# Attention, gated mix and feed-forward on one core: loads and dummy products ahead of the small vectors, a planner whose engines are free before their results, and later due times for gates and keys

## The chip, the cores and the metric

One Trainium2 chip, one core. Time is device microseconds (us) of one launch, the median of several runs; lower is better.

## The reference, cut to what matters

```python
# q, k, v: batch 2, 8 heads, 768 positions, head size 64; n_global 8, n_local 96
rel = pos[:, None] - pos[None, :]
keep = (pos[None, :] < n_global) | ((rel >= 0) & (rel < n_local))
scores = q @ k.T / 8 - slope_h * where(is_global & ~is_local, n_local, abs(rel))
a = softmax(where(keep, scores, -1e9)); x = a @ v          # 1536 tokens x 512
xk, xr = mu * x + (1 - mu) * x_prev                        # one mu for keys, one for gates
x = sigmoid(xr @ w_r) * (relu(xk @ w_k) ** 2 @ w_v)        # 512 -> 1024 -> 512
out = x + relu(layernorm(x) * g_ln @ w_ch1) @ w_ch2        # 512 -> 2048 -> 512
```

Weights are 64-bit floats. Each 128 x 512 piece is loaded as pairs of 32-bit words, turned into a 32-bit float and split into a high and a low part; the large products add high x high, high x low and low x high.

## The kernel before, in words

Tokens stand in 12 blocks of 128 (two batches of six). A block's attention is done in two halves of four heads, 24 half-blocks in all. In a block's first position the band of keys is 128 wide, elsewhere 232 (global 8, local 96, own 128). The steps of a half-block: transposition of q and k (`plan_turn`, L438; the copies out of PSUM are L445 on DVE, which multiplies by a scale tile `qs`, and L337 on ACT); scores (`plan_scores`, L484); adding the bias and taking the least (L495, DVE; it reads the bias tiles `nb0` or `nb`); exponent and sum (L501, ACT); transposition of the weights (`plan_weighted`, L519); one copy of them out of PSUM (L337 on ACT, tile `yy`); products with the values (L534). `plan_out` scales and transposes (L569). Then come, for six groups of 256 tokens, the gates' products (`plan_r`, L720, two halves of six per 128 tokens), the keys' products (`plan_k`, L756, eight of twelve), the values' products (`plan_v`, L793 to L795), and last the feed-forward half (L1047, L1141 to L1157).

Most work is recorded as operations with their engine, an estimated duration, what they read and write, the buffers they need and a due time. `Plan.play` then sets the order: it keeps a time for each engine (`CLOCK` holds the first ones), and always takes the operation that can start soonest by its estimates, the one with the earlier due time where several can. What it takes is issued at once, so it fixes every engine's instruction order, and the order of the loads on SP's queue. Its times steer nothing on the chip, where an engine goes on as soon as its semaphores let it.

The start is written by hand: eight memsets of `qs` and one of a 128 x 512 tile on POOL, ten dummy products on that tile (`warm_up`, L246), index tables on POOL (L265), the bias for the first block (`nb0`, L254 to L285, DVE, which needs the two counts that `words` loads), three loads of small vectors on SP's queue (L307). The bias for the other blocks (`nb`, L288 to L294) is one planned operation. `outside_band` (L67 to L87, twelve small DVE instructions) checks the counts; it is planned with a very late due time, and goes where DVE is free by the plan.

Of the kernel before, what the change touches and what calls it, by code (L numbers as in the profile page):

```python
# [8 lines left out]
F32 = mybir.dt.float32  # L9
F32R = mybir.dt.float32r  # L10
I32 = mybir.dt.int32
AF = mybir.ActivationFunctionType
ALU = mybir.AluOpType
# [3 lines left out]
P = 128  # L17
# [15 lines left out]

CLOCK = {"PE": 8.0, "ACT": 8.0, "DVE": 9.5, "POOL": 8.0, "SP": 2.5}
T0, STEP = 10.0, 5.0
CONV0, CONV1 = 20.0, 7.0
CONV2, CONV3 = 105.0, 5.0
K0 = 85.0  # L40
LOW, LATE_LOW = {"POOL": 1440}, {"DVE": 715}
TS = S // 2
PAIRS = 8
UP, LEAD = 15.6, 10.0
WARM = 10
SCALE = 0.125
BIG = 2.0**38
SM_EPS = 1e-9
# [7 lines left out]
def words(nc, a, tile_):  # L56

    w = tile_([P, 2, 2], "words", I32)
    for i, n in enumerate(("n_global", "n_local")):
        (nc.scalar, nc.gpsimd)[i].dma_start(w[:, i, :], a[n].bitcast(I32).rearrange("(o n) -> o n", o=1).to_broadcast([P, 2]))  # L60
    return w


# [46 lines left out]
class Plan:  # L110
# [4 lines left out]
    LAG = 70.0  # L115

    SWITCH = 95.0

    def __init__(self, clock):
        self.clock = {e: 1000.0 * t for e, t in clock.items()}  # L120
# [21 lines left out]
    def play(self):  # L142
# [13 lines left out]
        while open_:  # L156
            best = None
            for i in open_:
                engines, _, _, rooms, due, _, _ = self.ops[i]
                at = ready[i]  # L160
                ok = True
                for x in rooms:
                    if x.tile is None:
                        if live.get(x.tag, 0) < x.bufs:
                            f = free.setdefault(x.tag, [0.0] * x.bufs)
                            at = max(at, f[0])
                        else:
# [12 lines left out]
            t, _, i, e = best  # L180
            engines, fn, _, rooms, _, size, way = self.ops[i]
            for x in rooms:
                if x.tile is None:
                    live[x.tag] = live.get(x.tag, 0) + 1
                    free[x.tag].pop(0)
                    x.tile = x.make()
            self.now = t
            fn(e)
            end = t + engines[e]
            if e == "PE" and way != mode:  # L190
                end += self.SWITCH
                mode = way
            self.clock[e] = end
            if size:
                dma = max(dma, end) + size / 190.0
                end = dma + 1900.0
            trace.append((t, end, e, i))
            for x in rooms:
                x.left -= 1
                x.end = max(x.end, end)  # L200
                if not x.left and not x.hold:
                    live[x.tag] -= 1
                    free[x.tag].append(x.end + self.LAG)
# [11 lines left out]
class Fast:  # L215
# [23 lines left out]
    def warm_up(self):  # L239
# [1 line left out]

        ps = self.bank(7)
        y = self.t([P, 512], "cv", F32R, bufs=2)
        self.nc.gpsimd.memset(y.bitcast(F32), 1.0)
        for _ in range(WARM):
            self.nc.tensor.matmul(ps, y[:, 0:P], y, start=True, stop=True)  # L246

    def constants(self):
# [2 lines left out]

        nc = self.nc
        f = self.t([P, 2], "low")
        nc.vector.tensor_copy(f, self.words[:, :, 0])  # L254
        ng, nl = f[:, 0:1], f[:, 1:2]


# [18 lines left out]
        self.nb, self.nb0 = z[:, 0:C], z[:, C : C + P]  # L276
        o = slice(0, P)
        nc.vector.tensor_scalar(M[:, o], R[:, o], 0.0, None, ALU.is_ge)
        nc.vector.tensor_scalar(G0, J, ng, None, ALU.is_lt)
        nc.vector.scalar_tensor_tensor(L[:, o], R[:, o], nl, M[:, o], ALU.is_lt, ALU.mult)  # L280
        nc.vector.tensor_tensor(M0, G0, L[:, o], ALU.max)
# [4 lines left out]
        yield  # L286
        o = slice(P, C)
        nc.vector.tensor_scalar(M[:, o], R[:, o], 0.0, None, ALU.is_ge)  # L288
        nc.vector.scalar_tensor_tensor(L[:, o], R[:, o], nl, M[:, o], ALU.is_lt, ALU.mult)
        for x in firsts:  # L290
            nc.vector.tensor_scalar(L[:, x], R[:, x], ng, None, ALU.is_lt)
            nc.vector.tensor_scalar(R[:, x], R[:, x], 0.0, nl, ALU.mult, ALU.add)
        nc.vector.tensor_scalar(M, L, -BIG, BIG, ALU.mult, ALU.add)
        nc.vector.tensor_tensor(self.nb, R, M, ALU.add)  # L294

# [3 lines left out]
            self.nc.gpsimd.memset(self.qs[(h % 2) * D : (h % 2 + 1) * D, h // 2, :], -SCALE / slope(h))  # L299

    def small_params(self):
        nc, a = self.nc, self.a
        self.mhalf = self.t([P, 1], "mhalf")
        nc.vector.memset(self.mhalf, -0.5)
        self.vec = self.t([P, 5, 4], "vec")
        for i, n in enumerate(("moe_mu_k", "moe_mu_r", "moe2_g_ln")):
            nc.sync.dma_start(self.vec[:, i, :], a[n].rearrange("(c p) -> p c", p=P))  # L307
        nc.vector.tensor_scalar(self.vec[:, 3:5, :], self.vec[:, 0:2, :], -1.0, 1.0, ALU.mult, ALU.add)

    def part(self, tags):  # L310

# [151 lines left out]
    def plan_scores(self, i):  # L463
# [26 lines left out]
        for x, k in enumerate((0, 2, 1, 3)):  # L490
# [10 lines left out]
                nc.scalar.activation(t, t, AF.Exp, bias=mn.tile[:, k : k + 1], scale=-1.0, accum_out=sm.tile[:, h : h + 1])  # L501

            p.op({"DVE": 165 + 1.31 * w}, least, [("S", i), ("nb", n % NB > 0)], [("tp", i, k)], [tp, mn, banks[k % 2], self.bias], due + 1 + x)
            p.op({"ACT": 465 + 0.86 * w}, exp, [], [("tp", i, k), ("sm", n, h)], [tp, mn, sm], due + 1.5 + x)

    def plan_weighted(self, i):

# [141 lines left out]
    def plan_mix(self, g, m, rooms, put, cell, due, behind=()):  # L649
# [4 lines left out]
        for s in range(2):  # L654
# [21 lines left out]
                (nc.vector if e == "DVE" else nc.gpsimd).tensor_tensor(lo[:, c, :], y.tile, hi[:, c, :].bitcast(F32), ALU.subtract)  # L676

            Y = ("rt", cell, g, s)
            p.op({"POOL": 1200}, first, xs, [Y], [X, y] + rooms, due, behind=behind)
            p.op({"DVE": 1400}, second, xs, [Y], [X, y], due)  # L680
            p.op({"ACT": 630}, high, [Y], [(cell, g, s, 0)], [y] + rooms, due)
            p.op(LATE_LOW if g >= (EG if m else 1) else LOW, low, [Y, (cell, g, s, 0)], [(cell, g, s, 1)], [y] + rooms, due)

# [191 lines left out]
    def first(self, last):  # L875
# [10 lines left out]
        bias = self.constants()  # L886
        self.bias = Room("ln", 1, lambda: self.nb)
        with self.tc.manual_schedule(engines=ORDERED):
            self.query_scale()
            self.warm_up()  # L890
            next(bias)
            self.small_params()
            rooms = [self.token("rt", 2), self.token("rt", 2), self.token("e", 2)]
            p.op({"DVE": 2700}, lambda e: next(bias, None), (), [("nb", True)], rooms, self.due(1))
            for n in range(NBLK):
                self.plan_loads(n)
                self.plan_values(n)
# [8 lines left out]
                raw = Part([early], lambda t, j=j: t[:, j - 2]) if j in (2, 3) else None  # L906
                self.plan_weight(("m1", i), self.src[i], lambda i=i: self.place(i), CONV0 + CONV1 * j, raw=raw)
            for g in range(EG):
                self.plan_r(g, self.due(4 * g + 3) + 18)
            r3 = self.r_op  # L910
            self.plan_k(0, K0, K0 - 6)
            k0 = self.k_op
# [68 lines left out]
    def plan_w1(self, q, c, due, behind=()):  # L981
# [8 lines left out]
                y = cv.tile.bitcast(F32)[:, 2 * u * P : (2 * u + 2) * P]  # L990
                nc.scalar.activation(y, y, AF.Copy, scale=self.vec[:, 2, 2 * u + c : 2 * u + c + 1])

        p.op({"ACT": 840}, scale, [], [C], [cv], due)
        w = lambda k: raw.tile.rearrange("p n w -> p (n w)").bitcast(F32)[:, k * P : (k + 1) * P]
        y = lambda i, k0, k1: S.tile[:, 0:3584].rearrange("p (i c n) -> p i c n", i=2, c=2)[:, i, c, k0 * P : k1 * P]
        key = ("w1", q, c)
# [391 lines left out]
```

## Time and profile before

| | |
|---|---|
| median of 3 runs | 554.92 us (554.62 to 555.76) |
| profiled execution, its own time | 556.07 us |
| its span, first to last instruction | 554.2 us |
| TensorE (PE) busy | 528.0 us (95%) |
| VectorE (DVE) busy | 403.8 us (73%) |
| ScalarE (ACT) busy | 288.2 us (52%) |
| GpSimd (POOL) busy | 278.6 us (50%) |
| granted TensorE clock, mean | 0.989 |

Read it so: PE is busy nearly all the time, so a gain has to come from the 26 us in which PE does nothing, from PE time at the lower clock, or from less PE work. Busy shares of the other engines are means over stages that differ.

### The profile page before, as it was taken

The numbers are of one execution on the slowest core, as the hardware profiler recorded it, in microseconds if no ns is written. First come the engines' busy times: TensorE is split into PE (matmuls) and PEld (weight loads), VectorE is DVE, ScalarE is ACT, GpSimd is POOL, SyncE is SP. The second block draws the span as 40 slices with busy tenths as digits, with TensorE's granted clock in tenths as the row PEclk, the third lists the DMA queues.
The fourth block names the chain that finished last, engine by engine and source line by source line (L and its number), as shares of the span: only waits on it lengthen the run. The fifth ranks groups of instructions, "written<-read, shape, count | busy, mean of one in ns | idle before, by whom it ended". The sixth has DMA issues, their size and how long they took to land.

```text
span 554.2 us, 8779 instructions
## 1 busy us (share of the span) xinstructions
PE 528.0 (95%) x3178; PEld 454.2 (82%) x3178; DVE 403.8 (73%) x791; ACT 288.2 (52%) x641; POOL 278.6 (50%) x338
## 2 busy tenths in 40 slices
PE   5889999999999999999999999999999999999994
PEld 4667776887799898988888898788888889888983
DVE  4788799786597355828889987777676867867463
ACT  2687888777543313454446472473545526454320
POOL 3168575745545022151236592793855739585200
PEclk9699999999999999999999999999999999999999
DMA  8899667421310000020220123012130311311024
GB/s 168 205 229 192 150 157 176 146 69 53 101 38 2 1 2 0 1 72 5 77 69 8 52 63 95 20 64 90 45 109 0 115 39 43 110 38 39 0 77 157
DMA packets 59456, 42.64 MB, mean 77 GB/s; under 512 B 49036, under 2 KB 49292, under 8 KB 59404
## 3 DMA queue, kind: packets, MB, share of 16 engines
q1 hardware_dynamic: 58796, 41.33, 27.9%
q8 instruction: 27, 0.44, 0.3%
q10 hardware_dynamic: 576, 0.66, 0.3%
q14 instruction: 25, 0.20, 0.1%
q0 software_dynamic: 32, 0.00, 0.0%
HBM read 38.84 MB, written 3.15 MB: 76 GB/s over the span
## 4 chain that ended last, share of the span: by engine, by line


## 5 line engine op out<-in xcount | busy, mean ns | idle before, releaser
L1147 DVE TENSOR_TENSOR xg<-b,xg 128x1024 f32<-128x1024 f32 x44 | 53.6, 1219 | 39.5 <-PE b L1143 39.3
L595 DVE SCALAR_TENSOR_TENSOR cv<-cv,stage 128x512 int32<-128x512 int32 x50 | 43.9, 879 | 8.9 <-ACT cv L337 5.0
L594 DVE SCALAR_TENSOR_TENSOR stage<-stage 128x512 int32<-128x512 int32 x50 | 46.8, 938 | 0.6
L501 ACT ACTIVATE t0l<-t0l,mn 128x232 f32<-128x232 f32 (+1 forms) x96 | 44.5, 467 | 4.4 <-DVE mn L495 4.2
L1066 POOL TENSOR_TENSOR h<-rt,h 128x384 fp32r<-128x384 f32 x28 | 35.9, 1281 | 15.3 <-ACT h L337 15.3
L495 DVE CUSTOM_DVE_ANT_0 t0l<-b,ln 128x232 f32<-128x232 f32 (+1 forms) x96 | 32.0, 373 | 14.5 <-PE b L484 14.5
L664 POOL TENSOR_SCALAR rt<-xg,vec 128x256 f32<-128x256 f32 x48 | 29.9, 639 | 15.6 <-DVE m L771 4.3
L605 POOL TENSOR_TENSOR s<-cv,s 128x384 fp32r<-128x384 f32 (+1 forms) x22 | 26.8, 1217 | 19.0 <-ACT s L601 19.0
L1066 POOL TENSOR_TENSOR h<-e,h 128x384 fp32r<-128x384 f32 x14 | 15.9, 1134 | 38.2 <-ACT h L337 38.2
L831 POOL TENSOR_SCALAR st<-st 128x1 f32<-128x1 f32 x12 | 4.5, 375 | 60.2 <-DVE st L828 60.0
L756 PE MATMUL b<-b0l,t1l 128*128 128x256 f32 x144 | 32.6, 284 | 0.5 <-DVE rt L766 0.5
L593 DVE TENSOR_SCALAR stage<-stage 128x512 int32<-128x512 int32 x50 | 30.9, 620 | 2.8 <-DMA stage<-in_moe_w_v_dram 1.6
L519 PE MATMUL b<-ident,t0l 128*116 128x128 f32 (+1 forms) x176 | 30.1, 287 | 1.5 <-ACT t0l L501 1.5
L669 DVE SCALAR_TENSOR_TENSOR rt<-xg,vec,rt 128x256 f32<-128x256 f32 x48 | 29.1, 654 | 1.4 <-POOL rt L664 1.4
L1062 ACT ACTIVATE e<-e 128x384 f32<-128x384 f32 x16 | 8.3, 522 | 41.5 <-DVE e L1055 41.5
L534 PE MATMUL b<-yy,h 116*64 116x128 f32 (+1 forms) x352 | 25.0, 283 | 4.8 <-ACT yy L337 4.8
L1047 PE MATMUL b<-t1h,s 128*128 128x384 f32 x128 | 27.8, 339 | 0.6 <-DVE e L1055 0.6
L1062 ACT ACTIVATE rt<-rt 128x384 f32<-128x384 f32 x32 | 16.6, 520 | 22.6 <-DVE rt L1055 22.6
L534 PEld LDWEIGHTS b<-yy,h 116*64 116x64 f32 (+1 forms) x352 | 19.0, 138 | 11.2 <-ACT yy L337 8.6
L337 ACT ACTIVATE yy<-b 116x1024 f32<-116x1024 f32 (+1 forms) x24 | 22.8, 949 | 10.0 <-PE b L519 9.9
L1047 PE MATMUL b<-t0h,s 128*128 128x384 f32 x128 | 27.9, 339 | 0.0
L519 PEld LDWEIGHTS b<-ident,t0l 128*116 128x116 f32 (+1 forms) x176 | 20.1, 139 | 8.5 <-issue 3.8
(307 smaller groups left out, 1673.4 us busy)
## 6 DMA issues: line engine op xcount, KB each, us to landing
stage<-in_moe_w_ch_dram SPq DMA_DIRECT2D x32, 512.0 KB
stage<-in_moe_w_k_dram SPq DMA_DIRECT2D x8, 512.0 KB
stage<-in_moe_w_v_dram SPq DMA_DIRECT2D x8, 512.0 KB
h<-in_v_dram SPq DMA_DIRECT2D x10, 192.0 KB
b0l<-in_q_dram SPq DMA_DIRECT2D x7, 256.0 KB
out_dram<-xg SPq DMA_DIRECT2D x3, 512.0 KB
stage<-in_moe_w_r_dram SPq DMA_DIRECT2D x2, 512.0 KB
b0h<-in_q_dram SPq DMA_DIRECT2D x4, 256.0 KB
```

Source lines behind the costliest of these rows:

```text
L495: nc.vector.tensor_tensor_reduce(tp.tile[:, k, 0:w], S(k), bias, slope(h), 3.0e38, ALU.add, ALU.min, mn.tile[:, k : k + 1])
L501: nc.scalar.activation(t, t, AF.Exp, bias=mn.tile[:, k : k + 1], scale=-1.0, accum_out=sm.tile[:, h : h + 1])
L519: nc.tensor.transpose(b.tile[0:w, c, k * P : (k + 1) * P], tp.tile[:, k, c * w : (c + 1) * w], self.ident)
L534: nc.tensor.matmul(o, self.V[n].tile[0:w, c, h, :], y.tile[0:w, c, k * P : (k + 1) * P], start=c == 0, stop=c == m - 1)
L593: p.op({"DVE": 500}, lambda e: nc.vector.tensor_scalar(low(), low(), 29, None, ALU.logical_shift_right), [R], [(R, 1)], [raw], due - 2, be ...
L594: p.op({"DVE": 760}, lambda e: nc.vector.scalar_tensor_tensor(low(), high(), -(1 << 31), low(), ALU.bitwise_and, ALU.bitwise_or), [R, (R, ...
L595: p.op({"DVE": 760}, lambda e: nc.vector.scalar_tensor_tensor(y(), y(), 3, low(), ALU.logical_shift_left, ALU.bitwise_or), [(R, 2)], [C], ...
L664: nc.gpsimd.tensor_scalar(y.tile[:, u], z, v, 0.0, ALU.mult, ALU.add)
L756: nc.tensor.matmul(o, l, r, start=s == 0, stop=s == 11)
L1047: nc.tensor.matmul(acc(x), lhs(i, c, n), rhs(r, j, c), start=y == 0, stop=y == 5)
L1066: lambda e: (nc.vector if e == "DVE" else nc.gpsimd).tensor_tensor(o(1), V(y), o(0).bitcast(F32), ALU.subtract),
L1147: p.op({"DVE": 1250}, lambda e, x=x, z=rooms[0]: nc.vector.tensor_tensor(x(), z.tile.rearrange("p a n -> p (a n)"), x(), ALU.add), cells, ...
```

## The change

It moves parts of the start, changes constants of the planner and splits one planned operation. The small vectors' loads and the one instruction that reads them become planned operations; the second count is loaded by ACT's queue; the 128 x 512 memset goes from POOL to DVE, the memsets of `qs` behind the index tables, `mhalf` to POOL; nine dummy products for ten; `nb` in four parts; an engine's planned clock after an operation is set back by `OVERLAP`; due times of gates' products are 27 us later, of the first keys' products 30 us later.

```diff
-CLOCK = {"PE": 8.0, "ACT": 8.0, "DVE": 9.5, "POOL": 8.0, "SP": 2.5}
-T0, STEP = 10.0, 5.0
+CLOCK = {"PE": 5.2, "ACT": 3.0, "DVE": 6.2, "POOL": 4.0, "SP": 0.8}
+T0, STEP = 6.0, 5.0
-K0 = 85.0
+K0 = 115.0
-WARM = 10
+WARM = 9
@@ words
-        (nc.scalar, nc.gpsimd)[i].dma_start(w[:, i, :], a[n]...to_broadcast([P, 2]))
+        nc.scalar.dma_start(w[:, i, :], a[n]...to_broadcast([P, 2]))
@@ class Plan
+    OVERLAP = {"ACT": 105.0, "DVE": 85.0, "POOL": 120.0}
...
-            self.clock[e] = end
+            self.clock[e] = end - self.OVERLAP.get(e, 0.0)
@@ warm_up
-        self.nc.gpsimd.memset(y.bitcast(F32), 1.0)
+        self.nc.vector.memset(y.bitcast(F32), 1.0)
@@ constants
-        nc.vector.tensor_copy(f, self.words[:, :, 0])
...
         nc.vector.tensor_scalar(M[:, o], R[:, o], 0.0, None, ALU.is_ge)
+        nc.vector.tensor_copy(f, self.words[:, :, 0])
...
+        yield
...
@@ small_params
-        nc.vector.memset(self.mhalf, -0.5)
+        nc.gpsimd.memset(self.mhalf, -0.5)
...
-            nc.sync.dma_start(self.vec[:, i, :], a[n].rearrange("(c p) -> p c", p=P))
-        nc.vector.tensor_scalar(self.vec[:, 3:5, :], self.vec[:, 0:2, :], -1.0, 1.0, ALU.mult, ALU.add)
+            p.op({"SP": 500}, lambda e, i=i, n=n: nc.sync.dma_start(self.vec[:, i, :], a[n].rearrange("(c p) -> p c", p=P)), (), [("vec", i)], (), due - 18, size=P * 60)
+        p.op({"DVE": 200}, lambda e: nc.vector.tensor_scalar(self.vec[:, 3:5, :], ...), [("vec", 0), ("vec", 1)], [("vec", 3)], (), due)
@@ plan_scores
-            p.op({"ACT": 465 + 0.86 * w}, exp, ...)
+            p.op({"ACT": 385 + 0.86 * w}, exp, ...)
@@ first
-            self.query_scale()
             self.warm_up()
             next(bias)
+            self.query_scale()
             self.small_params()
-            p.op({"DVE": 2700}, lambda e: next(bias, None), (), [("nb", True)], rooms, self.due(1))
+            for ns in (350, 500, 800, 900):
+                p.op({"DVE": ns}, lambda e: next(bias, None), (), [("nb", True)], rooms, self.due(1))
...
-                self.plan_r(g, self.due(4 * g + 3) + 18)
+                self.plan_r(g, self.due(4 * g + 3) + 45)
```

**SP's queue at the start.** Before, its first rows (`vec` are the small vectors, `b0l` and `u` hold the first q and k):

```order
L307 DMA vec_121<-in_moe_mu_k_dram 128x4x1
L307 DMA vec_121<-in_moe_mu_r_dram 128x4x1
L307 DMA vec_121<-in_moe_g_ln_dram 128x4x1
L396 DMA b0l_126<-in_q_dram 128x4x64
L350 DMA u_128<-in_k_dram 128x4x64
L396 DMA b0l_126<-in_q_dram 128x4x64
L350 DMA u_128<-in_k_dram 128x4x64
```

and now:

```order
L404 DMA b0l_121<-in_q_dram 128x4x64
L358 DMA u_123<-in_k_dram 128x4x64
L404 DMA b0l_121<-in_q_dram 128x4x64
L358 DMA u_123<-in_k_dram 128x4x64
L404 DMA b0l_121<-in_q_dram 128x8x64
L355 DMA u_123<-in_k_dram 96x8x64
L356 DMA u_123<-in_k_dram 32x8x64
L416 DMA h_13_130<-in_v_dram 128x8x64
L598 DMA stage_132<-in_moe_w_r_dram 128x1024
L312 DMA vec_120<-in_moe_mu_k_dram 128x4x1
```

The first q and k are three places further up, the small vectors nine places further down.

**DVE between the first q and the first scores.** Before, from the small vectors to the first least (L495):

```order
L304 MEMSET mhalf_119 128x1
L308 TENSOR_SCALAR vec_121<-vec_121 128x8
L445 TENSOR_TENSOR b0l_126<-b_18_156,qs_76 128x256
L288 TENSOR_SCALAR rt_101<-rt_100 128x240
L289 SCALAR_TENSOR_TENSOR e_102<-rt_100,low_98,rt_101 128x240
L291 TENSOR_SCALAR e_102<-rt_100,low_98 128x8
...
L293 TENSOR_SCALAR rt_101<-e_102 128x368
L294 TENSOR_TENSOR ln_110<-rt_100,rt_101 128x368
L495 ISA t0l_190,mn_191<-b_21_180,ln_110 128x128
```

and now (L67 to L87 are `outside_band`):

```order
L453 TENSOR_TENSOR b0l_121<-b_18_154,qs_109 128x256
L289 TENSOR_SCALAR rt_90<-rt_89 128x240
L562 MEMSET xg_176 128x4
L562 MEMSET xg_178 128x4
L67 CAST counts<-words 128x2
...
L85 TENSOR_SCALAR inside<-counts 128x1
L87 CAST flag<-inside 128x1
L503 ISA t0l_201,mn_202<-b_21_170,ln_99 128x128
```

Most of `nb` has moved behind the first least instructions, and all of `outside_band` has moved in front of them.

**PE in the middle of attention,** half-blocks 12 and 13 of the 24. Before (L484 scores, L519 weights turned, L534 products with values, L438 q or k turned):

```order
L438 MATMUL b_149_1009<-ident,b0h_139 128x128 x4
L519 MATMUL b_151_1017<-ident,t0l_190 128x128
L534 MATMUL b_153_1022<-yy_228,h_13_135 64x128 x4
L519 MATMUL b_151_1017<-ident,t0l_190 128x128 x2
L484 MATMUL b_154_1033<-b0h_139,b0l_126 128x232
L484 MATMUL b_155_1034<-b0h_139,b0l_126 128x232
L484 MATMUL b_154_1033<-b0h_139,b0l_126 128x232
L484 MATMUL b_155_1034<-b0h_139,b0l_126 128x232
L519 MATMUL b_151_1017<-ident,t0l_190 128x128
L534 MATMUL b_153_1022<-yy_228,h_13_135 64x128 x4
```

and now:

```order
L542 MATMUL b_145_972<-yy_238,h_13_130 64x128 x4
L527 MATMUL b_146_979<-ident,t0l_201 128x128 x2
L492 MATMUL b_147_983<-b0h_137,b0l_121 128x232
L492 MATMUL b_148_984<-b0h_137,b0l_121 128x232
L492 MATMUL b_147_983<-b0h_137,b0l_121 128x232
L492 MATMUL b_148_984<-b0h_137,b0l_121 128x232
L527 MATMUL b_146_979<-ident,t0l_201 128x128 x2
L446 MATMUL b_150_995<-ident,b0h_137 128x128 x4
L728 MATMUL b_143_952<-s_36_242,h_67_446 128x512 x6
L542 MATMUL b_145_972<-yy_238,h_13_130 64x128 x4
```

Before, half-block 13's products with values (the last row) stood right behind its last transposition; now a transposition of q and half a gates' product stand between.

## Rows read from the trace of the kernel before

**Rows 1.** Windows: stretch, its length, each engine's busy time, PE's clock, DMA share, GB/s

```profile
4.01:8.45 4.44, 4.44 (x11) 3.36 (x11) 2.09 (x11) 0.00 (x0) 0.94 (x7) 1.00 1.13 209
8.45:12.57 4.12, 2.41 (x17) 1.55 (x15) 3.28 (x16) 1.53 (x6) 0.00 (x0) 1.00 1.15 263
12.57:22.81 10.24, 9.43 (x44) 6.53 (x44) 7.44 (x43) 5.08 (x20) 2.92 (x4) 0.50 0.94 203
22.81:46.40 23.59, 19.69 (x183) 14.72 (x184) 20.62 (x59) 20.62 (x59) 13.23 (x16) 1.00 0.98 206
46.40:148.30 101.90, 97.27 (x815) 77.47 (x813) 78.62 (x223) 78.70 (x213) 62.53 (x72) 1.00 0.51 129
148.30:541.00 392.70, 388.84 (x2089) 346.08 (x2088) 288.00 (x439) 180.94 (x347) 196.30 (x225) 1.00 0.15 47
```

**Rows 2.** Waits of PE from 0 to 150: in total, times, longest

```profile
PE b L534 <- ACT yy L337: 4.8, 8, 0.9
PE b L484 <- ACT b0h L337: 1.6, 3, 0.7
```

**Rows 3.** Timeline of the start: start us, us, engine, line, operation

```profile
0.74 0.45 SPq L307 DMA_DIRECT2D vec<-in_moe_mu_k_dram  x1
2.33 0.51 SPq L396 DMA_DIRECT2D b0l<-in_q_dram  x1
3.43 0.53 POOL L244 MEMSET cv<- 128x512 f32 x1
4.01 4.64 PE L246 MATMUL b<-cv 128*128 128x512 f32 x10 [4.01 <-POOL cv L244]
5.21 0.17 DVE L254 CAST low<-words 128x2 f32<-128x2 int32 x1 [5.21 <-DMA words<-in_n_local_dram]
6.99 0.29 DVE L285 TENSOR_TENSOR ln<-rt,rt 128x128 f32<-128x128 f32 x1
8.45 0.63 PE L438 MATMUL b<-ident,b0l 128*128 128x128 f32 x2
9.46 0.28 DVE L288 TENSOR_SCALAR rt<-rt 128x240 f32<-128x240 f32 x1
11.92 0.28 DVE L495 CUSTOM_DVE_ANT_0 t0l<-b,ln 128x128 f32<-128x128 f32 x1
17.94 0.16 DVE L67 CAST counts<-words 128x2 f32<-128x2 int32 x1
19.68 0.15 DVE L87 CAST flag<-inside 128x1 int32<-128x1 f32 x1
```

**Rows 4.** DMA from 0 to 16 us in 40 slices of 0.4 us; one load's landing

```profile
GB/s 0 0 0 0 0 3 3 5 2 2 65 126 221 275 239 244 211 245 247 232 198 188 199 204 207 207 245 358 373 348 288 260 232 228 237 202 321 348 432 236
words<-in_n_local_dram POOLq DMA_DIRECT2D x1, 1.0 KB, 3.9
```

**Rows 5.** Timeline of PE: half-block 3 turned, then its products with values; a gates' half

```profile
30.62 1.05 PE L484 MATMUL b<-b0h,b0l 64*128 64x232 f32 x8
31.60 0.65 PE L519 MATMUL b<-ident,t0l 128*116 128x128 f32 x4
32.09 0.60 PE L438 MATMUL b<-ident,u 128*128 128x128 f32 x4
33.42 1.09 PE L534 MATMUL b<-yy,h 116*64 116x128 f32 x16 [0.74 <-ACT yy L337]
...
46.48 1.64 PE L720 MATMUL b<-s,h 128*128 128x512 f32 x6
```

**Rows 6.** Timeline of PE: two starts of the first values' products (three make one)

```profile
149.13 0.39 PE L793 MATMUL b<-s,t0h 128*128 128x512 f32 x1
...
149.82 0.40 PE L793 MATMUL b<-s,t0h 128*128 128x512 f32 x1
```

**Rows 7.** The page's groups: a weight's last DVE step, and its low part on POOL

```profile
L595 DVE SCALAR_TENSOR_TENSOR cv<-cv,stage 128x512 int32<-128x512 int32 x50 | 43.9, 879 | 8.9 <-ACT cv L337 5.0
L605 POOL TENSOR_TENSOR s<-cv,s 128x384 fp32r<-128x384 f32 (+1 forms) x22 | 26.8, 1217 | 19.0 <-ACT s L601 19.0
```

More of the change, by code (lines that the diff above doesn't have):

```diff
@@ L59, in words @@
     for i, n in enumerate(("n_global", "n_local")):
-        (nc.scalar, nc.gpsimd)[i].dma_start(w[:, i, :], a[n].bitcast(I32).rearrange("(o n) -> o n", o=1).to_broadcast([P, 2]))
+        nc.scalar.dma_start(w[:, i, :], a[n].bitcast(I32).rearrange("(o n) -> o n", o=1).to_broadcast([P, 2]))
     return w
@@ L288, in constants @@
         nc.vector.tensor_scalar(M[:, o], R[:, o], 0.0, None, ALU.is_ge)
+        yield
         nc.vector.scalar_tensor_tensor(L[:, o], R[:, o], nl, M[:, o], ALU.is_lt, ALU.mult)
+        yield
         for x in firsts:
@@ L292, in constants @@
             nc.vector.tensor_scalar(R[:, x], R[:, x], 0.0, nl, ALU.mult, ALU.add)
+        yield
         nc.vector.tensor_scalar(M, L, -BIG, BIG, ALU.mult, ALU.add)
@@ L301, in small_params @@
     def small_params(self):
-        nc, a = self.nc, self.a
+        nc, a, p = self.nc, self.a, self.plan
         self.mhalf = self.t([P, 1], "mhalf")
-        nc.vector.memset(self.mhalf, -0.5)
+        nc.gpsimd.memset(self.mhalf, -0.5)
         self.vec = self.t([P, 5, 4], "vec")
+        due = self.due(4)
         for i, n in enumerate(("moe_mu_k", "moe_mu_r", "moe2_g_ln")):
-            nc.sync.dma_start(self.vec[:, i, :], a[n].rearrange("(c p) -> p c", p=P))
-        nc.vector.tensor_scalar(self.vec[:, 3:5, :], self.vec[:, 0:2, :], -1.0, 1.0, ALU.mult, ALU.add)
+            p.op({"SP": 500}, lambda e, i=i, n=n: nc.sync.dma_start(self.vec[:, i, :], a[n].rearrange("(c p) -> p c", p=P)), (), [("vec", i)], (), due - 18, size=P * 60)
+        p.op(
+            {"DVE": 200}, lambda e: nc.vector.tensor_scalar(self.vec[:, 3:5, :], self.vec[:, 0:2, :], -1.0, 1.0, ALU.mult, ALU.add),
+            [("vec", 0), ("vec", 1)], [("vec", 3)], (), due,
+        )
     def part(self, tags):
@@ L503, in plan_scores @@
             p.op({"DVE": 165 + 1.31 * w}, least, [("S", i), ("nb", n % NB > 0)], [("tp", i, k)], [tp, mn, banks[k % 2], self.bias], due + 1 + x)
-            p.op({"ACT": 465 + 0.86 * w}, exp, [], [("tp", i, k), ("sm", n, h)], [tp, mn, sm], due + 1.5 + x)
+            p.op({"ACT": 385 + 0.86 * w}, exp, [], [("tp", i, k), ("sm", n, h)], [tp, mn, sm], due + 1.5 + x)
     def plan_weighted(self, i):
@@ L678, in plan_mix @@
             Y = ("rt", cell, g, s)
-            p.op({"POOL": 1200}, first, xs, [Y], [X, y] + rooms, due, behind=behind)
-            p.op({"DVE": 1400}, second, xs, [Y], [X, y], due)
+            p.op({"POOL": 1200}, first, xs + [("vec", 3)], [Y], [X, y] + rooms, due, behind=behind)
+            p.op({"DVE": 1400}, second, xs + [("vec", m)], [Y], [X, y], due)
             p.op({"ACT": 630}, high, [Y], [(cell, g, s, 0)], [y] + rooms, due)
@@ L991, in scale @@
                 nc.scalar.activation(y, y, AF.Copy, scale=self.vec[:, 2, 2 * u + c : 2 * u + c + 1])
-        p.op({"ACT": 840}, scale, [], [C], [cv], due)
+        p.op({"ACT": 840}, scale, [("vec", 2)], [C], [cv], due)
         w = lambda k: raw.tile.rearrange("p n w -> p (n w)").bitcast(F32)[:, k * P : (k + 1) * P]
```

## The prediction

> **What bounds the kernel now.** I read the windows first. From 148.3 to 541 us PE is idle for 3.9 us of 392.7 (392.70 - 388.84), in the rest of attention (46.4 to 148.3) for 4.6 of 101.9, from 22.81 to 46.4 for 3.9 of 23.6, and in the first stretch after the dummies (8.45 to 12.57) for 1.7 of 4.1 [rows 1]. The reader is to see that the second half of the kernel can hardly be shortened by an order of instructions: there PE is the bound. [...] The list of waits then says which of the idle time is one thing: 4.8 us in eight waits of the products with values (L534) for ACT's copy of the turned weights [rows 2]. The timeline gives the rest: the start [rows 3] and one such wait in full [rows 5].
>
> **The start.** SP issues the three small vectors first, so the first q goes out at 2.33 instead of 0.74. POOL's memset ends at 3.96, the dummies begin at 4.01 and the first transposes of q stand right behind them at 8.45 [rows 3]. The bytes begin to flow in the slice at 4.0 us, 1.7 after q's issue. The first halves of q and k are 2 x 131 KB; the slices from there bring 26, 50, 88 and 110 KB (65, 126, 221 and 275 GB/s times 0.4 us), so both are there at about 5.6 [rows 4]. The dummies, not the loads, set the 8.45.
>
> In the changed kernel DVE makes the memset as its first instruction. A DVE memset of this shape is not in the trace: below it stands nothing, above it DVE's two-input pass over 512 elements with 0.88 [rows 7]; the nearest is POOL's of the same shape, 0.53, and I take 0.5. From 0.74, SP's first time, the dummies start at about 1.3. Ten took 4.44, so nine take 4.0 and end at 5.3 (4.8 to 5.7). The q and k, moved by 1.6, are there at 4.0; if the stream does not begin earlier after all, at 5.6. So the first transposes start at 5.3 and the start gains 3.15 us (2.8 to 3.6).
>
> Before q can be used DVE has to finish `nb0`: it waits for the counts until 5.21 and ends at 7.28, 2.07 of work. The second count now stands second on ACT's queue, issued at about 1.2 (0.45 for the one ahead). With POOL's 3.9 us to landing it comes at 5.1, and `nb0` ends at 7.2 instead of the 5.9 at which the turned q reaches DVE (5.3 and the 0.6 of two transposes): a loss of 1.3. But the small loads issued at 0.74 move bytes in the slice at 2.0, 1.3 after their issue [rows 4]; so it can be there at 2.5, and the loss be nothing. I take nothing and keep the 1.3. The index tables on POOL come earlier, since neither the word load nor both sorts of memset stand in front of them.
>
> Then DVE. Between 9.46 and 11.92 it works 2.46 us on `nb`, ahead of the first least [rows 3]. Now there stand one `nb` instruction (0.28), two tiny memsets, and `outside_band`, which took from 17.94 to 19.83, 1.89: together 2.3. The first least gains 0.2 more. Yet the other 2.2 us of `nb` now stand between the leasts of half-blocks 0 and 1 and ahead of the scaling of the second block's q, and the scores of block 1 queue behind that. Against that the 1.9 us of `outside_band` are gone from 17.94. I take a loss of 0.35 (0 to 1.3). **Start in all: -3.0 us** (-1.5 to -3.6).
>
> The vectors' loads go nine places down SP's queue, behind the first `w_r`; three issues at 0.5 each hold back the third block's q and k by no more than the 1.6 that everything behind them gained. Their DVE instruction stands behind half-block 1's leasts, and their first reader is the gates' mix, before the products that come at 46.48 [rows 5]. Cost nothing.
>
> **Attention's order.** In rows 5 the last four transpositions of half-block 3 end at 32.25 at the latest and its products with values start at 33.42. PE needs 1.17 us of other work there; it had one transposition of k (0.5) and waited 0.74. From the built order I counted, for each of the 24 half-blocks, the PE work between its last L519 and its first L534, at 0.5 for four transposes and 0.98 for scores (30.62 to 31.60). Before, eight have less than 1.17: five with 0.5, one with 1.0, two with nothing. The shortfalls are 5 x 0.67 + 0.17 + 2 x 1.17 = 5.9. The trace has eight such waits and 4.8 [rows 2], so the count overstates by a fifth (two blocks are narrower). After, five remain: two with nothing, one with 0.5, two with 1.0: 2 x 1.17 + 0.67 + 2 x 0.17 = 3.4, or 2.7 after the same discount. **-2.0 us** (0 to -3). The other waits, scores for ACT's copy of k with 1.6 [rows 2], go by the same sort of count: block 3 now has its scores right behind q's transposes, block 6 no longer. Nothing either way.
>
> Gates and keys are the filler. In the new order gates' products of group 3 (four halves of 1.6 [rows 5]) stand behind the last products with values, between the first `plan_v` steps, where nothing waits for ACT. Two weights of `w_v` are converted only after group 0's last keys' product. From there to their first use PE has an output's transposes, the values (1.0), four `plan_v` steps at 0.7 (149.13 to 149.82 [rows 6]) and two gates' halves: 0.5 + 1.0 + 2.8 + 3.2 = 7.5 us. The conversion needs an ACT copy, a DVE pass of 0.88, ACT's high part and POOL's low part of 1.22 [rows 7]; with 0.88 for each of ACT's, an estimate from DVE's pass over as many elements, 3.9 in series and 5.1 for the second weight. Covered; without that cover it would cost up to 5.1.
>
> `OVERLAP` and the shorter exponent change only estimates; what they do is in the order counted above. The order past 190 us differs in a few places with PE idle 3.9 us before, so I take 0 there (-1 to +1.5).
>
> **Sum.** -3.0 - 2.0 = -5.0. The profiled execution took 556.07, so 551.1 for one like it; its time is 1.15 above the median of the runs, and from the median 554.92 the same step gives **549.9 us**.
>
> [...]
>
> **Rivals.**
> - *Only the start counts* (0.18). The waits for ACT reappear at other places of the order, since ACT is busy 20.6 of 23.6 us between 22.81 and 46.4 [rows 1]. Then -3.0, between 551.3 and 553.3.
> - *The loads hold the first blocks* (0.12). From 4.8 us on the queues move 190 to 280 GB/s without a break [rows 4], and all loads but the first move by 1.6 us only. The start gives 1.6 or less, the order nothing: 553.3 to 555, no change that can be measured for most of it.
> - *The clock comes back late, slower* (0.10). From 22.81 to 46.4 PE is busy 83% at full clock. At half the clock it does 0.5 us of that work in 1 us and not 0.83, so each us of the half level beyond today's end costs 0.33/0.83 = 0.4 us. The gain of 5.0 is gone when it lasts 12.5 us longer, to about 35; it is slower by over 0.2% from 38 on, and if the level stays until the first gates' products at 46.48 it costs 9.5: 559. For it: the fall at 12.57 shows that this kind of work does not hold the level. Against: in the same stretch from 22.81 it held.
> - *More than that* (0.05): the clock does not fall at all. Half of 9.4 us is then saved at most, 4.7: down to 545.2.
>
> **How the numbers follow.** My forecast has 0.55, with a range of its own of 548 to 552. A measurement tells no change from one within 0.2%, so 553.8 to 556.0. Faster: 0.55 + 0.18 + 0.05 = 0.78; same 0.12; slower 0.10. The range of 547 to 554.3 leaves out the slower case, half of the loads' case and most of the last one.
>
> **What the next profile would show.** Right: dummies from about 1.3 and transposes of q at 5.3; the first least at about 8.5; the waits of L534 for ACT near 2.7 us in five or six places; the first `plan_v` product about 11 us earlier than 148.3 (5 of the gain and four gates' halves, 6.4, moved behind it), no PE idle time between there and the next keys' products. Wrong: a half level that lasts past 23 us, L445's first waiting for `words`, or as much PE idle time as before between 20 and 148.

## The result, and the profile after

The changed kernel takes 548.83 us (median of 4 runs, 548.58 to 549.63) where the kernel before takes 555.33 beside it (554.62 to 555.76): a ratio of 0.9884 [0.9868, 0.9899]. Run again on another occasion it took 549.12, ratio 0.9898 [0.9877, 0.9919]. The profiled execution took 548.74 with a span of 546.9 (before: 556.07 and 554.2), both at a mean granted clock of 0.989. In two variants below one execution was disturbed (1032 and 858 us), and no comparison uses it.

The windows of the changed kernel, cut at the same pieces of work: first transposes of q, first gates' product, the middle of the first full round of values, end of the keys, last down product, end; and, below the dots, the stretch at the half level. Columns as in [rows 1].

```profile
0.00:5.41 5.41, 3.97 (x10) 3.05 (x11) 0.72 (x3) 1.28 (x1) 2.49 (x22) 1.00 0.36 77
5.41:43.11 37.70, 30.45 (x241) 22.17 (x240) 30.68 (x119) 26.54 (x82) 15.77 (x21) 0.86 1.03 205
43.11:181.28 138.17, 135.87 (x1084) 114.50 (x1081) 112.34 (x276) 97.73 (x246) 79.27 (x95) 1.00 0.45 110
181.28:262.88 81.60, 81.50 (x505) 72.94 (x504) 50.63 (x95) 31.48 (x55) 19.43 (x32) 1.00 0.08 27
262.88:539.40 276.52, 271.10 (x1345) 241.25 (x1344) 207.69 (x299) 131.84 (x261) 155.93 (x168) 1.00 0.18 58
539.40:546.90 7.50, 0.80 (x4) 0.34 (x2) 0.93 (x3) 0.00 (x0) 0.00 (x0) 0.85 0.39 135
...
12.17:22.41 10.24, 9.08 (x47) 6.11 (x45) 7.43 (x31) 5.87 (x21) 2.38 (x4) 0.50 0.97 214
```

The kernel before, cut at the same work:

```profile
0.00:8.45 8.45, 4.44 (x11) 3.36 (x11) 2.09 (x11) 1.28 (x1) 3.66 (x23) 1.00 0.68 111
8.45:46.48 38.03, 31.60 (x245) 22.88 (x244) 31.43 (x114) 27.31 (x82) 16.23 (x20) 0.87 0.99 212
46.48:188.07 141.59, 136.96 (x1079) 114.05 (x1078) 109.50 (x272) 95.74 (x243) 80.75 (x98) 1.00 0.39 102
188.07:270.38 82.31, 81.86 (x505) 72.96 (x504) 51.84 (x95) 30.96 (x54) 22.21 (x34) 1.00 0.08 26
270.38:546.10 275.72, 272.31 (x1344) 240.61 (x1343) 207.98 (x299) 132.87 (x264) 155.79 (x164) 1.00 0.18 59
546.10:554.20 8.10, 0.86 (x4) 0.38 (x2) 0.95 (x3) 0.00 (x0) 0.00 (x0) 0.86 0.31 107
```

The lengths differ by -3.04, -0.33, -3.42, -0.71, +0.80 and -0.60, in all -7.30: the span's difference. The third line is the order's place: PE's idle time there falls from 4.63 (141.59 - 136.96) to 2.30; the other 1.1 of the 3.42 is PE's busy time, for nearly the same number of products (1079 and 1084). The half level (a granted clock of 0.50) lasts 10.24 us, as before (12.57 to 22.81 in [rows 1]).

The timeline of the changed kernel's start (against [rows 3]):

```profile
0.73 0.45 SPq L404 DMA_DIRECT2D b0l<-in_q_dram  x1
0.90 0.48 DVE L245 MEMSET cv<- 128x512 f32 x1 [0.90 <-PEq L1384]
1.19 0.45 ACTq L60 DMA_DIRECT2D words<-in_n_local_dram  x1
1.44 4.13 PE L247 MATMUL b<-cv 128*128 128x512 f32 x9 [1.44 <-DVE cv L245]
5.33 0.17 DVE L279 CAST low<-words 128x2 f32<-128x2 int32 x1 [3.79 <-DMA words<-in_n_local_dram]
5.41 0.38 PE L446 MATMUL b<-ident,b0l 128*128 128x128 f32 x2
7.32 0.42 DVE L453 TENSOR_TENSOR b0l<-b,qs 128x256 f32<-128x256 f32 x1
7.87 0.16 DVE L67 CAST counts<-words 128x2 f32<-128x2 int32 x1
9.61 0.15 DVE L87 CAST flag<-inside 128x1 int32<-128x1 f32 x1
9.68 0.28 DVE L503 CUSTOM_DVE_ANT_0 t0l<-b,ln 128x128 f32<-128x128 f32 x1
```

The dummies start at 1.44 and the transposes at 5.41. But the second count, issued at 1.19, ends DVE's wait only at 5.33, so that the turned q, there at 5.8, is scaled at 7.32. DVE then makes `outside_band`, and the first least comes at 9.68: 2.24 earlier than before, not 3.04.

PE's waits in the first 150 us of the changed kernel (against [rows 2]: in total, times, longest; the products with values are L542 now), and, below the dots, the longest from 140 us on:

```profile
PE b L542 <- ACT yy L345: 3.1, 6, 1.4
PE b L527 <- ACT t0l L509: 1.7, 1, 1.7
PE b L492 <- DVE b0l L453: 1.0, 1, 1.0
...
PE b L1150 <- DVE xg L1156: 3.5, 4, 1.0
```

The wait for `yy` falls from 4.8 in eight places to 3.1 in six; the first scores now wait 1.0 for the scaled q. The junction, in PE's timeline:

```profile
135.96 0.50 PE L801 MATMUL b<-s,t0h 128*128 128x512 f32 x1
...
137.47 1.54 PE L728 MATMUL b<-s,h 128*128 128x512 f32 x6
138.85 0.40 PE L801 MATMUL b<-s,t0h 128*128 128x512 f32 x1
...
146.47 0.52 PE L764 MATMUL b<-b0h,t1h 128*128 128x256 f32 x3
```

The values' first product comes 12.4 us earlier than the 148.3 of [rows 1], and the gates' products of group 3 stand between the values' without a wait.

### The profile page after: what moved, and what is told of

Read it like the earlier page. It is cut to its first block, busy times and chain, and to the rows that moved or that the text cites. A ratio compares the mean times of both kernels' runs of the same rounds, so it can differ in the third digit from the quotient of the medians.

```text
span 546.9 us, 8808 instructions
## 1 busy us (share of the span) xinstructions
PE 523.7 (96%) x3177; PEld 454.2 (83%) x3177; DVE 403.0 (74%) x791; ACT 288.9 (53%) x641; POOL 272.9 (50%) x337
## 3 DMA queue, kind: packets, MB, share of 16 engines
HBM read 38.84 MB, written 3.15 MB: 77 GB/s over the span
## 4 chain that ended last, share of the span: by engine, by line
## 5 line engine op out<-in xcount | busy, mean ns | idle before, releaser
L602 DVE SCALAR_TENSOR_TENSOR stage<-stage 128x512 int32<-128x512 int32 x50 | 43.9, 878 | 0.6
L1075 POOL TENSOR_TENSOR h<-rt,h 128x384 fp32r<-128x384 f32 x28 | 34.0, 1214 | 18.9 <-ACT h L345 18.9
L672 POOL TENSOR_SCALAR rt<-xg,vec 128x256 f32<-128x256 f32 x48 | 31.1, 664 | 20.7 <-DVE yy L779 8.9
L613 POOL TENSOR_TENSOR s<-cv,s 128x384 fp32r<-128x384 f32 (+1 forms) x22 | 25.4, 1156 | 15.4 <-ACT s L609 15.4
L677 DVE SCALAR_TENSOR_TENSOR rt<-xg,vec,rt 128x256 f32<-128x256 f32 x48 | 32.2, 719 | 0.4 <-POOL rt L672 0.3
L527 PE MATMUL b<-ident,t0l 128*116 128x128 f32 (+1 forms) x176 | 28.3, 284 | 2.5 <-ACT t0l L509 1.7
L542 PE MATMUL b<-yy,h 116*64 116x128 f32 (+1 forms) x352 | 25.4, 286 | 3.1 <-ACT yy L345 3.1
L492 PE MATMUL b<-b0h,b0l 64*128 64x232 f32 (+1 forms) x192 | 25.8, 389 | 1.6 <-DVE b0l L453 1.0
L542 PEld LDWEIGHTS b<-yy,h 116*64 116x64 f32 (+1 forms) x352 | 19.3, 140 | 9.3 <-ACT yy L345 5.5
```

The source lines that it names most:

```text
L527: nc.tensor.transpose(b.tile[0:w, c, k * P : (k + 1) * P], tp.tile[:, k, c * w : (c + 1) * w], self.ident)
L542: nc.tensor.matmul(o, self.V[n].tile[0:w, c, h, :], y.tile[0:w, c, k * P : (k + 1) * P], start=c == 0, stop=c == m - 1)
L602: p.op({"DVE": 760}, lambda e: nc.vector.scalar_tensor_tensor(low(), high(), -(1 << 31), low(), ALU.bitwise_and, ALU.bitwise_or), [R, (R, ...
L672: nc.gpsimd.tensor_scalar(y.tile[:, u], z, v, 0.0, ALU.mult, ALU.add)
L677: nc.vector.scalar_tensor_tensor(y.tile[:, u], z, v, y.tile[:, u], ALU.mult, ALU.add)
L1075: lambda e: (nc.vector if e == "DVE" else nc.gpsimd).tensor_tensor(o(1), V(y), o(0).bitcast(F32), ALU.subtract),
```

## The experiments

Each first line of a diff is the changed kernel's unless said otherwise. "Mean clock" is that of one execution: a kernel's executions differ in it, and with it in time (the start with the new clocks: 0.985 to 0.997, 555.6 to 551.8 us), so a table at the end of the experiments sets like beside like, as far as the clock's record allows.

**The two halves of the change, apart.** The start alone (loads, memset, dummies, parts of `nb`), with everything of the planner as before:

```diff
-CLOCK = {"PE": 5.2, "ACT": 3.0, "DVE": 6.2, "POOL": 4.0, "SP": 0.8}
-T0, STEP = 6.0, 5.0
+CLOCK = {"PE": 8.0, "ACT": 8.0, "DVE": 9.5, "POOL": 8.0, "SP": 2.5}
+T0, STEP = 10.0, 5.0
-K0 = 115.0
+K0 = 85.0
-    OVERLAP = {"ACT": 105.0, "DVE": 85.0, "POOL": 120.0}
+    OVERLAP = {"ACT": 0.0, "DVE": 0.0, "POOL": 0.0}
-            p.op({"ACT": 385 + 0.86 * w}, exp, ...)
+            p.op({"ACT": 465 + 0.86 * w}, exp, ...)
-                self.plan_r(g, self.due(4 * g + 3) + 45)
+                self.plan_r(g, self.due(4 * g + 3) + 18)
```

> The hand-written start of the change (loads, memset on DVE, nine dummies, small vectors and bias parts planned) with the planner's constants and due times of before. Theory (start 3.0 us, and each us by which PE work behind a half-block's last transposition falls short of 1.17 us costs 0.8 us): the first transposes of q at 5.4, shortfalls counted from the built order 6.7 us against 5.9 before and 3.4 after, so 3.0 - 0.7 = 2.3 us faster than before, 553.0. Rival (the start carries all of the gain, the plan only shuffles): about 549. Rival (loads bind): under 1.6 us faster.

558.55 us, ratio 1.0083 [1.0059, 1.0108]: slower than before, though the first transposes start at 5.19. Part of that is the clock: all six executions have a mean of 0.983 to 0.986, and the profiled one is at the half level twice (granted 0.52 from 32.5 to 39.3 us, 0.54 from 66.0 to 73.4). Its waits of PE up to 190 us:

```profile
PE b L542 <- ACT yy L345: 4.1, 7, 1.3
PE b L577 <- DVE b0l L453: 3.8, 1, 3.8
PE b L577 <- POOL xg L570: 2.2, 2, 1.6
```

The counted waits are not the trouble; one wait of 3.8 us, of an output's transposes queued where DVE's scaling of q is late, is new. The planner's first clocks were those of the old start.

The order alone, in the kernel before (`OVERLAP`, 385, `K0` 115 and +45 there, nothing else):

> The start of before with the planner's OVERLAP, shorter exponent and later due times; first clocks and T0 stay as before. Theory: shortfalls 4.7 against 5.9 before, so 1.0 us faster than before, 554.3; waits of the products with values for ACT near 3.8 us. Rival (the start carries all): 555.3, no change.

553.24 us, 0.998 [0.9966, 0.9995]; 2.9 us of waits for `yy` in five places, but 2.9 at the first turning of weights, in a run whose half level lasted from 13.3 to 27.0.

The start with the new clocks and first time, the order as before:

```diff
-K0 = 115.0
+K0 = 85.0
-    OVERLAP = {"ACT": 105.0, "DVE": 85.0, "POOL": 120.0}
+    OVERLAP = {"ACT": 0.0, "DVE": 0.0, "POOL": 0.0}
-            p.op({"ACT": 385 + 0.86 * w}, exp, ...)
+            p.op({"ACT": 465 + 0.86 * w}, exp, ...)
-                self.plan_r(g, self.due(4 * g + 3) + 45)
+                self.plan_r(g, self.due(4 * g + 3) + 18)
```

> The new start and the plan's new clocks and first time alone: the planner's engines are not free ahead of their results, an exponential costs 465 again, and the first keys' and the gates' products are due when they were before. Waits of PE for the copy yy counted from the order: 6.9 us, as in the kernel before. Theory (the start's 3 us are kept, the order's 2 us are not): 551.5 to 552.5. Rival (the start's gain is eaten by a plan in which one attention chain after another is alone on PE, as in the start alone with the old clocks): 556 or more.

554.22 us, 0.9984 [0.9968, 1.0001]: between both forecasts (the kernel before counts 5.9, not the 6.9 said there). The new clocks are worth 4.3 us against the start alone in the medians and some 3 at like mean clock (0.985 to 0.986: 558.0 to 559.8 against 555.3 to 555.6). Even with them the start by itself is worth only 0.5 us in the medians.

**Parts of the order, undone in the changed kernel.** The due times:

```diff
-K0 = 115.0
+K0 = 85.0
-                self.plan_r(g, self.due(4 * g + 3) + 45)
+                self.plan_r(g, self.due(4 * g + 3) + 18)
```

> The changed kernel with the due times of gates' and first keys' products as before. Theory: shortfalls 6.8 against 3.4, so 2.7 us slower than the changed kernel, 551.5, and those waits near 5.4 us. Rival (start carries all): 548.8 to 549.3.

552.75 us, 0.9967 [0.9947, 0.9986]. `OVERLAP` alone (three zeros in its place):

> The changed kernel, where the planner alone no longer lets ACT, DVE and POOL begin their next operation ahead of a result's end; the exponential's cost of 385, the new clocks and due times stay. Waits for yy counted from the order: 5.9 us against 3.4. The first gates' product stands at place 72 of PE's attention and gates work (57 in the changed kernel, 98 in the run that undid the exponential's cost too). Theory (the counted waits are what an order costs): 551.3. Rival (what costs is that gates' products come late, so that attention chains stand alone on PE): between 551 and 563.9 by their place, some 556.

555.95 us, 0.9997 [0.9968, 1.0025], the rival's number. The rival's mechanism is not shown by it: the first gates' product comes at 48.5 us here and at 42.8 in the start alone, which has more idle time (table below). `OVERLAP` and the exponential's cost (465) together:

> The changed kernel with OVERLAP zero and the exponent's estimate as before. Theory: shortfalls 9.3 against 3.4, so 4.7 us slower than the changed kernel, 553.5, those waits near 7.4 us. Rival (start carries all): 548.8 to 549.5. If it is slower by less than 2 us the count of shortfalls is no measure.

563.85 us, 1.0169 [1.0137, 1.0201], 10 us more than the theory; the first gates' product comes at 65.2 us instead of 43.1. So the part that I had called a change of estimates carries most. Each profiled run's waits for `yy`, the same as counted from the order, PE's idle time from the first transposes to the middle of the values (length less busy time, from windows), and its own time; the last column is the median of the kernel's runs:

| kernel | waits for `yy` | counted | idle, that stage | profiled run | median |
|---|---|---|---|---|---|
| before | 4.8 | 5.9 | 11.1 | 556.1 | 555.3 |
| order alone | 2.9 | 4.7 | 9.8 | 554.8 | 553.2 |
| start alone | 4.1 | 6.7 | 16.9 | 559.8 | 558.6 |
| start, new clocks | 5.7 | 6.9 | 13.2 | 553.0 | 554.2 |
| due times undone | 4.8 | 6.8 | 11.1 | 552.5 | 552.8 |
| `OVERLAP` undone | 5.0 | 5.9 | 11.9 | 551.4 | 556.0 |
| and exponential's cost | 6.9 | 9.3 | 18.4 | 560.0 | 563.9 |
| changed | 3.1 | 3.4 | 9.5 | 548.7 | 548.8 |

The waits for `yy` are a tenth to two fifths less than counted, in every row. The count doesn't foretell the idle time, of which they are a quarter to under a half. Nor is the idle time all that an order costs: where two profiled runs show no half level from 8 us on, the stage is 177.1 us with `OVERLAP` undone and 172.0 in the variant with the late mask (below), whose planned order is the changed kernel's; 3.0 of these 5.1 us are idle time, 2.1 busy time for the same 1322 products. What makes that busy time is not shown.

**Is the start still on the path?** The changed kernel was run again, with three edits of it beside it.

> The changed kernel once more, on the chip of the three runs beside it, so that they can be compared with it: 548.8 us, ratio 0.988 to 0.991; first transposes at 5.41 us, first least score at 9.68 us, 3.1 us of waits for the copy yy in the first 150 us.

549.12 us, 0.9898 [0.9877, 0.9919]: as forecast. Three more dummies:

```diff
-WARM = 9
+WARM = 12
```

> Twelve dummy products in place of nine, nothing else moved: they end at about 6.7 us, past the landing of the tokens, and the first transposes start then, 1.3 us later than in the changed kernel. Theory (what the start gains or loses is carried to the end): 1.0 to 1.3 us above the control, about 550. Rival (the small vectors end after the transposes and set the first least score at 9.68 us whatever the dummies do, so that the start has room): 0 to 0.4 us above the control. If the ratio to the control differs by over 3 us, then a plan that suits the durations is worth more than the start itself.

548.60 us (median of five), 0.986 [0.9828, 0.9893]. The transposes start at 6.73, the first least at 9.82 (9.54 in the run of the control), and nothing is lost: the rival. DVE's small instructions (`nb0` behind the counts, then `outside_band`) set the first least, not the dummies. `outside_band` moved to the plan's first values:

```diff
-                lambda e, tb=tb, ev=ev: nc.vector.scalar_tensor_tensor(x1.tile[...], ev(), 1.0, acc(tb), ALU.add, ALU.mult),
+                lambda e, tb=tb, ev=ev: (nc.vector.scalar_tensor_tensor(x1.tile[...], ev(), 1.0, acc(tb), ALU.add, ALU.mult), self.late() if (g, tb) == (0, 1) else None),
...
-            p.op({"DVE": 3000}, lambda e: last(), due=at[NG] + 150)
+            p.op({"DVE": 3000}, lambda e: None, due=at[NG] + 150)
```

> The mask of the band's outside is built at the plan's first values (some 170 us) and not at the start; its planned place of 3000 ns stays empty and the order of all else is unchanged. Theory: the first least score comes 1.0 to 1.9 us earlier (about 8.3 from 9.68), and the time falls by 1.0 us against the control, to about 547.8. Rival: the halves after it are bound by the products of the other half-blocks, the time stays within 0.3 us of the control.

548.28 us (median of five), 0.9873 [0.9839, 0.9907]. The first least comes at 8.42, 1.1 earlier than the control's, and where the clock is like the control's the time is 548.3 to 548.7 against 548.6 to 549.0: the rival. And with the local count first on SP's queue:

```diff
-        nc.scalar.dma_start(w[:, i, :], a[n]...to_broadcast([P, 2]))
+        (nc.scalar, nc.sync)[i].dma_start(w[:, i, :], a[n]...to_broadcast([P, 2]))
```

> As the run before, and the word of the tokens' count is loaded first on SP's queue, not second on ScalarE's. Theory: it lands at about 4 us and not at 5.2, the small vectors end at 6 and the first least score comes at 7.5 to 8; q lands up to 0.5 us later. Against the control 1.5 us less, about 547.3. Rival: what the vectors gain is lost to q's later landing, and the time is that of the run before.

548.19 us, 0.9853 [0.9822, 0.9884]. DVE's wait now ends at 4.93, by the other count. Both edits of DVE's start together are worth half a microsecond at the most (548.2 against 548.6 at a clock of 0.987): transposes 1.3 us later, or a first least 1.1 us earlier, did not move the end. What went with shorter times was the clock: five executions of these three variants took 544.5 to 544.7 at a mean of 0.996 to 0.998, none of the changed kernel's ten did (0.984 to 0.989).

**Holding the clock.** Products of the dummies' kind among attention's first steps, to try whether PE's waits there have a part in the fall to the half level. Three stand in the wait ahead of the first turning of weights; ahead of the second and the third, one each, PE did not wait in the changed kernel:

```diff
+FILL = {0: 3, 1: 1, 2: 1}
...
+        self.ones = y
         for _ in range(WARM):
...
             def turn(e, k=k):
+                for _ in range(FILL.get(i, 0) if k == 0 else 0):
+                    nc.tensor.matmul(b.tile[:, 0], self.ones[:, 0:P], self.ones, start=True, stop=True)
                 for c in range(m):
```

> The changed kernel, with five more dummy products of 512 columns in PE's first waits (three ahead of the first half's turning of weights, one each ahead of the second's and the third's), in places where it waits 1.67, 0 and 0.69 us. [...] Theory B (the fall is not set by these waits): the time is 548.5 to 549.5, up to 0.6 us worse for what the dummies delay.

545.18 us (544.76 to 546.53, 5 runs), 0.983 [0.9807, 0.9852]: not theory B, but inside the 544.5 to 545.5 that the author expected should filling these waits keep the level up. (The 0.69 of the forecast is a wait of the products with values, not of the third turning.) The interval lies below those of the changed kernel, which was run on other occasions. Its windows:

```profile
5.41:12.17 6.76, 5.09 (x36) 3.31 (x34) 6.09 (x39) 3.25 (x14) 0.00 (x0) 1.00 1.15 217
12.17:22.41 10.24, 8.42 (x78) 6.26 (x78) 9.69 (x36) 8.23 (x27) 3.38 (x5) 1.00 0.96 207
...
5.45:17.00 11.55, 8.85 (x67) 5.97 (x67) 10.85 (x58) 6.16 (x23) 0.90 (x3) 1.00 1.23 213
```

From 12.17 to 22.41 PE makes 78 products in 8.42 us of work, where the changed kernel makes 47 in 9.08, the clock at 1.00 and at 0.50. The second profiled run of the changed kernel is the closest pair: in both the clock is up by 7.1 us (two transposes in 0.41, against 0.62 to 0.66 before). First the changed kernel, then the filled one:

```profile
7.07 0.41 PE L446 MATMUL b<-ident,u 128*128 128x128 f32 x2 [0.54 <-ACT b0h L345]
10.41 0.48 PE L527 MATMUL b<-ident,t0l 128*128 128x128 f32 x1 [1.67 <-ACT t0l L509]
10.82 1.23 PE L492 MATMUL b<-b0h,b0l 64*128 64x128 f32 x8
...
7.12 0.41 PE L448 MATMUL b<-ident,u 128*128 128x128 f32 x2 [0.55 <-ACT b0h L347]
8.52 0.94 PE L529 MATMUL b<-cv 128*128 128x512 f32 x3
10.44 0.33 PE L531 MATMUL b<-ident,t0l 128*128 128x128 f32 x1 [0.98 <-ACT t0l L511]
10.70 0.72 PE L494 MATMUL b<-b0h,b0l 64*128 64x128 f32 x8
```

With 1.67 us of waiting the scores behind it take 1.23 us, as at the half level (1.23 too with twelve dummies at 10.97, where the column gives 0.72 from 10 to 12 us and 0.50 from 12 on); with three products in that wait they take 0.72. The occasion alone doesn't explain it: the start with new clocks and the kernel with `OVERLAP` undone, run beside the filled one, have a mean clock under 0.990 in seven of their twelve executions each, the filled one in none of five. The same in the variant with the late mask, one dummy for the three:

```diff
+FILL = {0: 1, 1: 1, 2: 1}
```

> The variant with the late mask and the words on SP's queue, with three more dummy products (one each ahead of the first three halves' turning of weights). [...] Theory B: 548.2 in the median, two in six near 544.6.

547.02 us (544.48 to 548.16), 0.9845 [0.9817, 0.9873]: two of six near 544.6 and three above 548, as theory B has it; the median lies between its 548.2 and the 544 to 545 expected for most runs should filling keep the level up. Its profiled run shows why, and below the dots that of the variant without the fill:

```profile
5.45:17.00 11.55, 10.30 (x50) 6.91 (x49) 8.17 (x39) 4.73 (x18) 0.64 (x1) 1.00 1.14 211
14.01 1.12 PE L546 MATMUL b<-yy,h 128*64 128x128 f32 x8 [0.69 <-ACT yy L347]
20.09 0.66 PE L546 MATMUL b<-yy,h 128*64 128x128 f32 x8
...
5.45:17.00 11.55, 9.55 (x48) 6.34 (x47) 8.35 (x39) 4.72 (x17) 0.64 (x1) 1.00 1.23 214
```

50 products in 10.30 us, where the first filled kernel has 67 in 8.85 (its row below the dots): PE was slow from 5.5 us on, before any filling, although the clock's column prints 1.00. By the durations of its products the clock came up between 16.9 and 18.2 us (16 products in 2.94 us of work from 14 to 17, 23 in 3.00 from 17 to 20), and in the variant without the fill (549.18 us) between 20.4 and 21.8 (14 in 3.00 from 17 to 20, 25 in 3.00 from 20 to 23), behind the same nine dummies as in the changed kernel. In the first filled kernel's profiled run, where two transposes took 0.41 at 7.12, the column stays at 1.00 up to 43 us; here the fill did not bring the level up before 16.9.

Times by the mean clock of the execution (lowest to highest; -: none):

| kernel | 0.987 to 0.989 | 0.996 to 0.998 |
|---|---|---|
| before, beside the filled kernel | 555.8 to 557.7 | 553.3 to 554.4 |
| order alone | 552.8 to 553.3 | - |
| start, new clocks | 554.2 to 554.7 | 551.8 to 553.2 |
| due times undone | 552.2 to 552.8 | 548.5 |
| `OVERLAP` undone | 555.7 | 551.1 to 552.9 |
| and exponential's cost | 563.8 to 563.9 | 560.0 |
| changed (both occasions) | 548.6 to 549.0 | - |
| twelve dummies | 548.6 to 549.0 | 544.7 |
| late mask | 548.3 to 548.7 | 544.7 |
| late mask, count on SP | 548.2 | 544.5, 544.7, 549.2 |
| the same, three more dummies | - | 544.5, 544.6, 548.0 to 548.2 |
| filled | - | 544.8 to 545.2 |

The last column is not in every row like beside like. The mean doesn't show a slow start: the profiled executions of 549.2 and 548.0 us, with means of 0.996 and 0.997, are those whose products were slow until some 21 and 17 us. None of the eleven executions with filling has a mean under 0.990.

## Why the prediction was right

The sign, the range and nearly the time (549.9 forecast, 548.83 measured) were right; the sum of two terms is right in part by luck, as the fifth point says. The rivals *only the start counts* and *the loads hold the first blocks* are out: every execution of the changed kernel took under 550.2. (The second read [rows 4] as 190 to 280 GB/s from 4.8 us on; from 10.8 us on the row goes up to 432.) The parts:

- **Dummies and transposes.** 1.3 and 5.3 forecast, 1.44 and 5.41 measured; the gain of 3.15 is 3.04.
- **"I take nothing and keep the 1.3"** failed. The count landed 4.1 us after its issue, near POOL's 3.9 of [rows 4] and not the 1.3 of the small loads, so the first least came at 9.68, not 8.5. The forecast's own sign of being wrong, L445's first behind `words`, came true. It cost nothing that can be measured: one edit moved the transposes by 1.3 us and one the first least by 1.1 at the same total. The 0.35 for `nb`'s later parts can't be told apart from that.
- **The start in all, -3.0,** holds in the trace as far as the first transposes, and does not hold by itself. With the plan's old order and new clocks it gives 0.5 us in the medians and 1 to 2 at like clock; in the profiled run 2.1 of its 3 us are back as PE's idle time in attention (13.2 against 11.1).
- **The order, -2.0,** was mis-sized by its way of counting. Its waits fell nearly as counted (3.1 in six places; 2.7 in five or six forecast), and the idle time from 43 to 181 us by 2.3. But on top of the new start the order is worth 5.4 us (554.2 less 548.8). There the waits for `yy` fall by 2.6 (5.7 to 3.1) and the idle time of the stage by 3.7 (13.2 to 9.5): waits set at "nothing either way" move too, and the rest is not idle time of that stage. Undoing `OVERLAP`, which with the shorter exponent was to "change only estimates", costs some 7 us alone, undoing the due times 3.8 at like clock.
- **The sum** came out because the two errors are of opposite sign, which is luck. At a mean clock of 0.987 to 0.989, each beside the kernel before on its own occasion, the order alone gives some 2.5 us, the start with its clocks some 2, both together some 7: they are not additive, as the sum supposed. That the plan's first clocks must fit the start is shown (558.6 with the old ones, 554.2 with the new, some 3 us of it at like clock); what makes the other 2 to 3 us is open, since the idle time is spread over many small waits and part of the gain is busy time.
- **Past 190 us, 0** forecast: -0.71, +0.80 and -0.60 measured, inside the bounds. In the stretch of the +0.80 PE's idle time grows by 2.0 and its busy time falls by 1.2; the largest wait there, of L1150 for DVE, is 3.5 us in four places, where the kernel before has 1.5 for the same four. The junction cost nothing, as forecast.
- **The clock.** In the changed kernel's two profiled runs it was up behind the nine dummies (two transposes in 0.41 at 7.25 and at 7.07) and fell again, as in the kernel before. That was not always so, though: two variants with the same nine were profiled as slow as at the half level until some 17 and 21 us (eight products in 1.12 us at 14.0, as in the changed kernel at 13.25 under 0.50). The rival's price stands: 0.4 us for each us at the half level was worked out, and the fall costs 4.0 where one kernel ran both ways (twelve dummies: 548.6 to 549.0, with 10.2 us at the half level in the profiled run, against 544.7). The last rival, no fall at all, was put at 545.2, with 4.7 us saved from 549.9; the filled kernel takes 545.18, but saves 3.7 to 3.9 from 548.83 and 549.12. With five more products, three of them in a wait of 1.67 us, the fall is gone from its profiled run (1.00 from 12.17 to 22.41, where the changed kernel has 0.50). What sets the level is not shown: why it was up behind the same nine dummies in one execution and not in another is not explained by any run here.

## What to carry to other kernels

Where a planner sets the order, a shorter start and a better order are one change: the plan's first clocks have to move with the start, and each is to be tried with and without the other. A count of one kind of wait foretells that kind and not the idle time of the engine, and idle time is not all that an order costs, so price an order by the length of its stage. And before shaving the start, look at the granted clock behind it: here five needless products gave some 3.8 us on top of the changed kernel, where the moved start by itself gave 0.5 to 2.

## What the runs showed of the hardware

- The granted clock of the same kernel falls to 0.50 for some 10 us (10.24 in the profiled runs before and after) in some executions and not in others. By their mean clock (under 0.990) it is 7 of 12 for the start with new clocks and all ten of the changed kernel; when filled, one of five is in between (546.53 at a mean of 0.990). By the table above it is worth 2 to 5 us, as much as the edits that were to be told apart.
- The clock column can print 1.00, and the mean clock 0.997, where PE is as slow as under 0.50: in the second filled kernel 50 products in 10.30 us of busy time, eight of them in 1.12 us at 14.01, as in the changed kernel at 13.25 under 0.50. The count of products against their busy time shows it.
- Behind nine dummies from 1.44 to 5.65 us PE was not always at its later pace: in two profiled executions eight products of the same shape still took 1.12 us at 14.0; in the one with filling they took 0.66 at 20.09.
- A 1 KB load spread over 128 partitions, issued second on ACT's queue at 1.19 us, ended its reader's wait at 5.33.
